# A gated MLP on one core: the early weights' queue, the way of the first products back into their banks, and the order of the operand sums

## The chip, the cores and the metric

The kernel runs on one core of a Trainium2 chip. The core has TensorE (PE, matrix products; its weight loads are shown as PEld), VectorE (DVE), ScalarE (ACT), GpSimd (POOL) and SyncE (SP), which here only issues DMAs. Each engine works through its own instructions in program order, and semaphores tie them together. The metric is the device time of one execution in microseconds (us), from the first to the last instruction with what lies around them. The kernel before took 557.13 us, the median of 3 runs (556.48 to 557.19).

## What is computed

```python
# x: [1, 2048, 1024]   w_gate, w_up: [1024, 3584]   w_down: [3584, 1024]   all bf16
g = jnp.einsum("bsd,df->bsf", x, w_gate)
u = jnp.einsum("bsd,df->bsf", x, w_up)
h = gelu(g) * u                      # tanh form of gelu
out = jnp.einsum("bsf,fd->bsd", h, w_down)
```

## The kernel before

**Tiling.** The 2048 rows are done in two passes of 1024 (`NPASS`). In a pass the rows form two column halves `xT[0]` and `xT[1]` of 512 rows each, transposed, with the 1024 input features in eight blocks of 128 (`ko`). The 3584 hidden features form 28 blocks of 128, and two blocks make a unit: 14 units a pass. After the units of a pass, `down` multiplies by w_down.

**Seven products instead of eight.** A unit is a 2 x 2 by 2 x 2 block product: two feature blocks by two halves of the weights' inner dimension, against two such halves of x by two row halves. It is computed in Strassen's manner (Winograd's form) with seven products, for gate and up each. The operands of four of them are sums: of weights (`s1` to `s4`, `sa`, made by `sums_s`) and of x (`t1` to `t4`, `tb`, made by `sums_t`); `sa` and `tb` are casts by ScalarE. A product is four matmuls of 128 x 512 (`product`), so the five products of sums in `unit` are 40 matmuls for gate and up. The other two products take raw bf16 operands: the first, p1, uses the lower half of the inner dimension; the second is added to p1 in its bank and gives the block c11 directly, of which ScalarE's gelu and VectorE's multiplication (`times`) make one quarter of the unit's h. A copy of p1 is kept, because p1 is also part of the unit's other blocks.

**Banks.** PSUM has eight banks, used in four pairs (gate and up): E, K, C and F. In `unit` the first pair `e` takes the product s2 by t2; p1 has to be added to it. ScalarE copies the sum out as u2, then the product s3 by t3 is added to the bank, and so on. `c[i]` and `d` take the others; `p5` is ScalarE's copy of s1 by t1. For the units 0 to 5 of the first pass line 229 adds the kept p1 on VectorE; the other units find p1 in the bank already, because their raw products run in it.

```python
   225          for i in GU:
   226              product(e[i], s["s2"][i], t["t2"], p1 is not None)
   227          if p1:
   228              for i in GU:
   229                  dve(e[i], e[i], p1[i], ADD)
```

In the first pass u2 and p5 are stored over `xT[1]` (`spare0`), so they also wait until t2, t3 and tb have been made from it.

**The early units.** The first 40 us are laid out by hand (lines 484 to 569). Before `xT[1]` has arrived, PE can only do the two raw products of units 0 to 5, which need `xT[0]` and three weight blocks: `wa[0]` (units 0 and 1), `wa[2]` (2 and 3) and `wa[4]` (4 and 5). The sums of weights of these units need `wa[1]`, `wa[3]` and `wa[5]` as well. A weight block is 1 MB, two DMAs of 512 KB (gate and up). `xT[0]` is loaded plainly and transposed by PE (`turn`, four of them, each copied out of a bank), and `xT[1]` is loaded by eight transposing DMAs of 128 KB (`transposing`, line 476). Everything is issued on SP's queue, in this order: half of x's first rows, `wa[0]` in four slices with the other half of x between, `wa[2]`, four transposes, `wa[4]`, `wa[1]`, four transposes, `wa[3]`, `wa[5]`.

**The orders around the change.** PE, VectorE, GpSimd and SP keep the order of the program text everywhere, and so does ScalarE within the blocks under `manual_schedule`. The early block runs `early_p1` (first raw product), `early_snap` (ScalarE copies p1 out), `early_p2` (second raw product) and `early_c11` (gelu and multiplication), for units 0 and 1, then 2 and 3, then 4 and 5. Between them VectorE makes t1, s1, s2 (while GpSimd makes s3), then t2 and t3, and after the last c11 s4 and t4. `pool_behind` gives GpSimd a copy of one column of the last t3 tile, so that it starts on unit 1's sums only when t3 is done; `nxt = {"s": make_s(early[1], pool)}` are those sums. From then on GpSimd makes each unit's sums one unit ahead (`prepare`). VectorE meets unit 0's two additions of line 229 only after t4, since they stand behind it in the program.

**Names in the profile.** A bank shows as `bank`, the operands of sums as `s` and `t`, a copy of p1 as `p`. Copies over `xT[1]` show as `xT`, early data kept in the space of h as `hT` (among them `wa[3]` to `wa[5]`). Helpers give their line to all that they record: L91 is every VectorE sum, L94 every GpSimd sum, L108 every `snap`, L103 every `cast`, L115 every product, L127 every weight load, L194 every gelu.

Of the kernel before, what the change touches and what calls it, by code (L numbers as in the profile page):

```python
# [10 lines left out]
def kernel(  # L11
# [23 lines left out]
    nc = tc.nc  # L35
# [15 lines left out]
    NKB = Dm // P  # L51
# [8 lines left out]
    R = 6  # L60
# [29 lines left out]
    def dve(out, a, b, op):  # L90
        nc.vector.tensor_tensor(out=out, in0=a, in1=b, op=op)  # L91
# [29 lines left out]
    def new_w():  # L121
        return wpool.tile([P, 2, NKB, 2 * P], bf16, name="w")

    def load_w(n, w, k0=0, k1=NKB):
        f0 = n * 2 * P
        for i, src in enumerate((w_gate, w_up)):
            nc.sync.dma_start(  # L127
                out=w[:, i, k0:k1],
                in_=src[k0 * P : k1 * P, f0 : f0 + 2 * P].rearrange(
                    "(ko ki) f -> ki ko f", ki=P  # L130
                ),
            )
        return w
# [66 lines left out]
    def product(ps, lhs, rhs, start):  # L200
        for k in range(KH):
            matmul(ps, lhs[:, k, :], rhs[k], start and k == 0, k == KH - 1)
# [16 lines left out]
        g, up = add(c, p1)  # L219
        times(fb, 0, gelu(g), up)  # L220

    def unit(fbs, banks, s, t, p1, spare, after_p5, aside, keep, ahead_of_p4, behind_p4):
        GU = range(2)
        e, c, d = banks
        for i in GU:
            product(e[i], s["s2"][i], t["t2"], p1 is not None)
        if p1:
            for i in GU:
                dve(e[i], e[i], p1[i], ADD)
        aside()  # L230
        keep(0, c[0])
        u2 = [snap(e[i], "u2", spare[i]) for i in GU]
        keep(1, c[0])
        keep(2, c[1])
        up = c[1]
        c = d
        for i in GU:
            product(c[i], s["s1"][i], t["t1"], True)
        p5 = [snap(c[i], "p5", spare[2 + i]) for i in GU]
        after_p5()  # L240
        for i in GU:
            product(e[i], s["s3"][i], t["t3"], False)
        g = new(dve, e[0], p5[0], ADD, "sum", dtype=f32)
        dve(up, e[1], p5[1], ADD)
        for i in GU:
            product(c[i], s["s4"][i], t["tb"], False)
        times(fbs[1], 1, gelu(g), up)
        g, up = add(c, u2)
        times(fbs[0], 1, gelu(g), up)
        ahead_of_p4()  # L250
        for i in GU:
            product(e[i], s["sa"][i], t["t4"], False)
        behind_p4()
        times(fbs[1], 0, gelu(e[0]), e[1])
# [205 lines left out]
    def turn(ps, half, a, parts):  # L460
        tp = ps.bitcast(bf16).rearrange("p (k r) -> p k r", k=KH)
        for t in range(2):
            for k in range(KH):
                nc.tensor.transpose(
                    tp[:, k, t * P : (t + 1) * P], xn[half, a][:, t, k * P : (k + 1) * P], ident
                )
        n = KH // len(parts)
        for m, put in enumerate(parts):
            ks = slice(m * n, (m + 1) * n)
            put(  # L470
                out=xT[0][:, half * KH : (half + 1) * KH, a * 2 * P : (a + 1) * 2 * P][:, ks],
                in_=tp[:, ks],
            )

    def transposing(xT, c, ko, r0):
        nc.sync.dma_start_transpose(  # L476
            out=xT[c][:, ko, :], in_=x2[r0 : r0 + N, ko * P : (ko + 1) * P]
        )
# [7 lines left out]
    load_w(0, wa[0], 0, 2)  # L486
    load_w(0, wa[0], 2, 4)
    load_x(1)
    load_w(0, wa[0], 4, 6)
    load_w(0, wa[0], 6, 8)  # L490
    load_w(2, wa[2])
    for ko in range(KH):
        transposing(xT, 1, ko, N)
    load_w(4, wa[4])
    load_w(1, wa[1])
    for ko in range(KH, NKB):
        transposing(xT, 1, ko, N)
    load_w(3, wa[3])
    load_w(5, wa[5])
# [1 line left out]
    seen = xpool.tile([P, 1], f32, name="seen")  # L501
    E, K, C, F = odd, cc, dd, even
    s, t = sums_s(early[0], dve), sums_t(xT)
    s_pool = sums_s(early[0], pool)
    p1s = {}

    def early_p1(u, ps, i, ks, cols=slice(0, N)):
# [19 lines left out]
    def early_c11(u, ps):  # L527
        times(block(0, u, 0), 0, gelu(ps[0]), ps[1])

    with tc.manual_schedule(engines={ENG.Activation}):  # L530
        for _ in range(NWARM):
            nc.tensor.matmul(bank[3], lhsT=warm[:, :P], rhs=warm, start=True, stop=True)
        turn(bank[4], 0, 0, (on_dve,))
        turn(bank[5], 0, 1, (on_dve, on_act))
        pairs = [(u, ps, i) for u, ps in ((0, E), (1, K)) for i in range(2)]
        for cols in (slice(0, 2 * P), slice(2 * P, N)):
            for u, ps, i in pairs:
                early_p1(u, ps, i, range(0, 2), cols)
        for u, ps, i in pairs:
            early_p1(u, ps, i, range(2, KH))  # L540
        turn(bank[6], 1, 0, (on_dve,))
        turn(bank[7], 1, 1, (on_dve,))
        early_snap(0, E)
        early_snap(1, K)
        for ks in (range(0, 2), range(2, KH)):
            for u, ps, i in pairs:
                early_p2(u, ps, i, ks)
        early_c11(0, E)
        early_c11(1, K)
        for us in (((2, C), (3, F)), ((4, E), (5, K))):  # L550
            for u, ps in us:
                for i in range(2):
                    early_p1(u, ps, i, range(KH))
                early_snap(u, ps)
            if us[0][0] == 2:
                t.make("t1")
                s_pool.make("s3")
                s["s3"] = s_pool["s3"]
                s.make("s1", "s2")
            else:  # L560
                t.make("t2", "t3", "tb")
            for u, ps in us:
                for i in range(2):
                    early_p2(u, ps, i, range(KH))
                early_c11(u, ps)
        s.make("s4", "sa")
        t.make("t4")
        pool_behind(t["t3"][-1])
        nxt = {"s": make_s(early[1], pool)}
    spare0 = [as_f32(xT[1][:, 2 * m : 2 * m + 2]) for m in range(4)]  # L570

# [17 lines left out]
    for ip in range(NPASS):  # L589
        with tc.manual_schedule(engines={ENG.Activation}):  # L590
            if ip == 0:
                ws = {}
            else:
                raw_of(0, F)()
                raw_of(1, C)()
            for u in range(NU):
                js = making(u) if ip == 0 else []

                def prepare():
                    if "s" not in nxt and u + 1 < NU:  # L600
                        nxt["s"] = make_s(weights(ip, u + 1), pool)
                    if len(js) == 1:
                        store_made(js[0])
                    for j in js[1:]:
                        keep_whole(j)
                    if ip == 0:
                        fetch_wd(making(u + 1))

                def keep(part, ps):
                    if js:  # L610
                        keep_part(js[0], part, ps)

                def aside():
                    if u + 2 < NU:
                        weights(ip, u + 2)

                def ahead_of_p4():
                    if u % 2 and u + 1 < NU and (ip or u + 1 >= R):
                        raw_of(u + 1, F)()
                        nxt["c11"] = raw_of(u + 2, C)  # L620

                def behind_p4():
                    if "c11" in nxt:
                        nxt.pop("c11")()

                if u % 2 and (ip or u):
                    E, K, C = C, E, K
                banks = (E, K, C) if u % 2 else (F, K, E)
                unit(
                    [block(ip, u, h) for h in range(2)], banks, s, t,  # L630
                    p1s.pop(u) if ip == 0 and u < R else None,
                    [None] * 4 if ip else spare0,
                    prepare, aside, keep, ahead_of_p4, behind_p4,
                )
                s = nxt.pop("s", None)

        last = ip == NPASS - 1
        got, nxt = {}, {}

        def more(step):  # L640
            if last:
                return
            if step in (-1, 0, 2):
                store_made({-1: NJ - 3, 0: NJ - 2, 2: NJ - 1}[step])
            if step == 0:
                xT[:] = new_x()
            if step >= 24 and step % 2 == 0 and step // 2 - 12 < len(moves):
                c, ko = moves[step // 2 - 12]
                transposing(xT, c, ko, (2 * (ip + 1) + c) * N)
            if step == 50:  # L650
                ws.clear()
                loaded(0), loaded(1)
            if step == 58:
                got["s"] = make_s(loaded(0), dve)
            if step == 62:
                got["t"] = make_t(xT)

        down(ip, F + K, C + E, last, more)
        E, K, C, F = K, E, F, C
        if not last:  # L660
            t, s = got["t"], got["s"]
# [29 lines left out]
```

## Time and profile before

| what | value |
|---|---|
| median of 3 runs | 557.13 us (556.48 to 557.19) |
| the profiled execution's own time | 557.8 us |
| its span, first to last instruction | 556.0 us |
| mean granted clock of PE | 0.988 of full |
| PE busy | 537.0 us, 97%, 2380 matmuls |
| VectorE busy | 351.4 us, 63% |
| ScalarE busy | 265.5 us, 48% |
| GpSimd busy | 251.2 us, 45% |
| bytes moved | 93.29 MB, mean 168 GB/s |
| chain that ended last | PE 89%, VectorE 3%, SP's queue 3%, DMA 3% |

Busy times are for the whole span; what a stage is limited by has to be read from that stage's own rows. The profile cuts the span into 40 slices (13.9 us each) and gives each engine's busy share as a digit in tenths. A timeline row has the start, the time from the first start to the last end of the merged instructions, engine, line, operation, what is written and read, and the count; in brackets stands how long the engine had been idle before and what released it. A row `SPq` is the issue of a DMA, not its transfer. A row of waits has the total, the number of times and the longest.

### The profile page before, as it was taken

What the parts mean: (1) busy time and instruction counts of PE and PEld (TensorE: products, weight loads), DVE (VectorE), ACT (ScalarE), POOL (GpSimd) and SP (SyncE); (2) the same over time, 40 slices, a digit from 0 to 9 for tenths busy, and PEclk for the clock granted to TensorE, in tenths of its full rate; (3) what the DMA queues carried; (4) which work ended last, traced back from release to release, by engine and by line L of the source; (5) the groups of instructions that cost most, each with busy time, mean ns of one, the idle gap of its engine ahead of it and who ended that gap; (6) DMA issues with size and microseconds to landing.
All of it is one profiled execution on the core that took longest, in us unless ns stands there. A gap on an engine that the chain in (4) does not pass through costs nothing.

```text
span 556.0 us, 7452 instructions
## 1 busy us (share of the span) xinstructions
PE 537.0 (97%) x2380; PEld 386.2 (69%) x2399; DVE 351.4 (63%) x530; ACT 265.5 (48%) x471; POOL 251.2 (45%) x223
## 2 busy tenths in 40 slices
PE   8956999999999999999999999999999999999997
PEld 4434887686776864788877686867677686478886
DVE  1396787776776788478676546455455548866730
ACT  3523666676666631044535555645555552114541
POOL 0149997868776040000029776677777700000000
PEclk9986999999999999999999999999999999999999
DMA  9960059674846499999958242222222029662751
GB/s 235 209 161 17 23 176 259 170 217 132 265 126 209 141 367 386 292 251 215 282 180 212 65 107 77 76 77 77 77 76 77 1 80 382 239 219 87 222 194 56
DMA packets 108744, 93.29 MB, mean 168 GB/s; under 512 B 17313, under 2 KB 94113, under 8 KB 108705
## 3 DMA queue, kind: packets, MB, share of 16 engines
q1 hardware_dynamic: 108704, 92.82, 57.9%
q8 instruction: 19, 0.31, 0.3%
q14 instruction: 21, 0.16, 0.1%
HBM read 74.45 MB, written 15.20 MB: 161 GB/s over the span
## 4 chain that ended last, share of the span: by engine, by line
PE 89%; DVE 3%; SPq 3%; DMA 3%; issue 1%; ACT 0%; DVEq 0%; ACTq 0%
PE bank L115 89%; DVE t L91 2%; SPq L127 2%; DMA w<-in_w_up_dram 1%; SPq L476 1%; DMA raw<-in_w_down_dram 1%; DVE s L91 1%; DVE m L91 0%; DVE hT L91 0%; SPq L453 0%; ACT xT L108 0%; DVE bank L91 0%; ACT bank L281 0%; ACT st L422 0%; SPq L292 0%
## 5 line engine op out<-in xcount | busy, mean ns | idle before, releaser
L94 POOL TENSOR_TENSOR s<-w 128x512 fp32r<-128x512 bf16 x90 | 107.6, 1213 | 172.2 <-PE bank L115 100.2
L115 PE MATMUL bank<-t,s 128*128 128x512 f32 x672 | 161.4, 396 | 11.6 <-ACT xT L108 9.5
L115 PEld LDWEIGHTS bank<-t,s 128*128 128x128 f32 x672 | 127.8, 191 | 40.5 <-POOL s L94 10.4
L115 PE MATMUL bank<-xT,w 128*128 128x512 bf16 (+1 forms) x412 | 89.9, 375 | 2.2 <-DVE xT L470 1.0
L91 DVE TENSOR_TENSOR hT<-g,bank 128x512 bf16<-128x512 f32 x112 | 76.6, 688 | 18.8 <-ACT g L194 7.4
L194 ACT ACTIVATE g<-sum 128x512 f32<-128x512 f32 x78 | 49.5, 635 | 72.1 <-DVE sum L91 71.7
L108 ACT COPY p<-bank 128x512 f32<-128x512 f32 x96 | 54.6, 590 | 46.3 <-PE bank L115 45.8
L115 PEld LDWEIGHTS <-w 128*128 128x128 bf16 x424 | 40.4, 98 | 50.1 <-issue 4.1
L91 DVE TENSOR_TENSOR sum<-bank,p 128x512 f32<-128x512 f32 x36 | 24.9, 692 | 75.9 <-PE bank L115 75.9
L115 PE MATMUL bank<-q 128*128 128x512 f32 x240 | 58.9, 389 | 0.0
L115 PE MATMUL bank<-t,sa 128*128 128x512 f32 x224 | 57.5, 398 | 0.0
L115 PE MATMUL bank<-tb,s 128*128 128x512 f32 x224 | 56.4, 395 | 0.0
L94 POOL TENSOR_TENSOR s<-s,w 128x512 fp32r<-128x512 f32 x48 | 55.7, 1180 | 0.0
L94 POOL TENSOR_TENSOR s<-w,s 128x512 fp32r<-128x512 bf16 x48 | 55.7, 1181 | 0.0
L115 PEld LDWEIGHTS bank<-q 128*128 128x128 f32 x240 | 45.0, 188 | 9.4
L115 PEld LDWEIGHTS bank<-tb,s 128*128 128x128 f32 x224 | 42.8, 192 | 9.4 <-issue 0.3
L115 PEld LDWEIGHTS bank<-t,sa 128*128 128x128 f32 x224 | 42.1, 188 | 9.6
L115 PE MATMUL bank<-raw,hT 128*128 128x512 bf16 x218 | 48.4, 379 | 0.3
L103 ACT CAST tb<-raw 128x512 fp32r<-128x512 bf16 x28 | 17.3, 627 | 62.4 <-DMA raw<-in_w_down_dram 26.9
L115 PEld LDWEIGHTS <-hT 128*128 128x128 bf16 x256 | 24.8, 98 | 31.1 <-DMA hT<-in_w_up_dram 1.1
L108 ACT COPY xT<-bank 128x512 f32<-128x512 f32 x56 | 31.3, 589 | 23.3 <-DVE bank L91 18.1
L91 DVE TENSOR_TENSOR q<-hT 128x512 fp32r<-128x512 bf16 x56 | 38.4, 686 | 4.4 <-PE bank L115 4.4
(54 smaller groups left out, 539.5 us busy)
## 6 DMA issues: line engine op xcount, KB each, us to landing
raw<-in_w_down_dram SPq DMA_DIRECT2D x76, 256.0 KB, 5.0
q<-td SPq DMA_DIRECT2D x60, 256.0 KB, 5.0
w<-in_w_gate_dram SPq DMA_DIRECT2D x24, 512.0 KB, 5.7
w<-in_w_up_dram SPq DMA_DIRECT2D x24, 512.0 KB, 6.9
td<-m SPq DMA_DIRECT2D x12, 768.0 KB, 4.5
w<-td SPq DMA_DIRECT2D x6, 1024.0 KB, 9.9
out_dram<-st SPq DMA_DIRECT2D x32, 128.0 KB, 1.7
hT<-in_w_gate_dram SPq DMA_DIRECT2D x3, 512.0 KB, 5.5
```

Source lines behind the costliest of these rows:

```text
L91: nc.vector.tensor_tensor(out=out, in0=a, in1=b, op=op)
L94: nc.gpsimd.tensor_tensor(out=out, in0=a, in1=b, op=op)
L103: nc.scalar.copy(out=t, in_=src)
L108: nc.scalar.copy(out=t, in_=ps)
L115: nc.tensor.matmul(ps, lhsT=lhs, rhs=rhs, start=start, stop=stop, skip_group_check=True)
L127: nc.sync.dma_start(out=w[:, i, k0:k1], in_=src[k0 * P : k1 * P, f0 : f0 + 2 * P].rearrange("(ko ki) f -> ki ko f", ki=P),)
L194: nc.scalar.activation(g, src, ACT.Gelu_apprx_tanh)
L476: nc.sync.dma_start_transpose(out=xT[c][:, ko, :], in_=x2[r0 : r0 + N, ko * P : (ko + 1) * P])
```

## The change

Four things are edited. (1) The second half of `wa[0]`, and `wa[2]`, `wa[1]` and `wa[4]` whole, are issued by ScalarE (`queue=nc.scalar`), at four places between its copies and gelus; a one-column copy of x into `seen` makes ScalarE wait for the first x before the first of them. On SP the eight transposes follow each other directly behind x, then come `wa[3]` and `wa[5]`. (2) The turns of x's second half stand between PE's first products, and ScalarE takes half of the last one's copy. (3) The add of p1 in units 0 to 5 is dropped. A new function `seed` lets ScalarE copy p1 into the bank `e` ahead, for unit 0 at the end of the early block and for units 1 to 5 in the unit before, and the product is added to it. (4) s3 of unit 0 is made by VectorE and no longer by GpSimd; t3 and tb follow unit 4's c11; s3, s4, sa and t4 follow unit 5's; the call of `pool_behind` goes.

```diff
@@ -121,10 +121,10 @@
     def new_w():
         return wpool.tile([P, 2, NKB, 2 * P], bf16, name="w")
 
-    def load_w(n, w, k0=0, k1=NKB):
+    def load_w(n, w, k0=0, k1=NKB, queue=nc.sync):
         f0 = n * 2 * P
         for i, src in enumerate((w_gate, w_up)):
-            nc.sync.dma_start(
+            queue.dma_start(
                 out=w[:, i, k0:k1],
                 in_=src[k0 * P : k1 * P, f0 : f0 + 2 * P].rearrange(
                     "(ko ki) f -> ki ko f", ki=P
@@ -219,14 +219,11 @@
         g, up = add(c, p1)
         times(fb, 0, gelu(g), up)
 
-    def unit(fbs, banks, s, t, p1, spare, after_p5, aside, keep, ahead_of_p4, behind_p4):
+    def unit(fbs, banks, s, t, spare, after_p5, aside, keep, ahead_of_p4, behind_p4):
         GU = range(2)
         e, c, d = banks
         for i in GU:
-            product(e[i], s["s2"][i], t["t2"], p1 is not None)
-        if p1:
-            for i in GU:
-                dve(e[i], e[i], p1[i], ADD)
+            product(e[i], s["s2"][i], t["t2"], False)
         aside()
         keep(0, c[0])
         u2 = [snap(e[i], "u2", spare[i]) for i in GU]
@@ -486,14 +483,7 @@
     load_w(0, wa[0], 0, 2)
     load_w(0, wa[0], 2, 4)
     load_x(1)
-    load_w(0, wa[0], 4, 6)
-    load_w(0, wa[0], 6, 8)
-    load_w(2, wa[2])
-    for ko in range(KH):
-        transposing(xT, 1, ko, N)
-    load_w(4, wa[4])
-    load_w(1, wa[1])
-    for ko in range(KH, NKB):
+    for ko in range(NKB):
         transposing(xT, 1, ko, N)
     load_w(3, wa[3])
     load_w(5, wa[5])
@@ -501,7 +491,6 @@
     seen = xpool.tile([P, 1], f32, name="seen")
     E, K, C, F = odd, cc, dd, even
     s, t = sums_s(early[0], dve), sums_t(xT)
-    s_pool = sums_s(early[0], pool)
     p1s = {}
 
     def early_p1(u, ps, i, ks, cols=slice(0, N)):
@@ -527,26 +516,38 @@
     def early_c11(u, ps):
         times(block(0, u, 0), 0, gelu(ps[0]), ps[1])
 
+    def seed(u, e):
+        for i in range(2):
+            nc.scalar.copy(out=e[i], in_=p1s[u][i])
+
+    on_queue = nc.scalar
     with tc.manual_schedule(engines={ENG.Activation}):
         for _ in range(NWARM):
             nc.tensor.matmul(bank[3], lhsT=warm[:, :P], rhs=warm, start=True, stop=True)
+        nc.scalar.copy(out=seen, in_=xn[0, 0][:, 0, :1])
+        load_w(0, wa[0], 4, 8, on_queue)
         turn(bank[4], 0, 0, (on_dve,))
         turn(bank[5], 0, 1, (on_dve, on_act))
+        load_w(2, wa[2], queue=on_queue)
         pairs = [(u, ps, i) for u, ps in ((0, E), (1, K)) for i in range(2)]
         for cols in (slice(0, 2 * P), slice(2 * P, N)):
             for u, ps, i in pairs:
                 early_p1(u, ps, i, range(0, 2), cols)
-        for u, ps, i in pairs:
+        for u, ps, i in pairs[:2]:
             early_p1(u, ps, i, range(2, KH))
         turn(bank[6], 1, 0, (on_dve,))
-        turn(bank[7], 1, 1, (on_dve,))
+        early_p1(*pairs[2], range(2, KH))
+        turn(bank[7], 1, 1, (on_dve, on_act))
+        early_p1(*pairs[3], range(2, KH))
         early_snap(0, E)
         early_snap(1, K)
+        load_w(1, wa[1], queue=on_queue)
         for ks in (range(0, 2), range(2, KH)):
             for u, ps, i in pairs:
                 early_p2(u, ps, i, ks)
         early_c11(0, E)
         early_c11(1, K)
+        load_w(4, wa[4], queue=on_queue)
         for us in (((2, C), (3, F)), ((4, E), (5, K))):
             for u, ps in us:
                 for i in range(2):
@@ -554,18 +555,18 @@
                 early_snap(u, ps)
             if us[0][0] == 2:
                 t.make("t1")
-                s_pool.make("s3")
-                s["s3"] = s_pool["s3"]
                 s.make("s1", "s2")
             else:
-                t.make("t2", "t3", "tb")
+                t.make("t2")
             for u, ps in us:
                 for i in range(2):
                     early_p2(u, ps, i, range(KH))
                 early_c11(u, ps)
-        s.make("s4", "sa")
+                if u == 4:
+                    t.make("t3", "tb")
+        seed(0, F)
+        s.make("s3", "s4", "sa")
         t.make("t4")
-        pool_behind(t["t3"][-1])
         nxt = {"s": make_s(early[1], pool)}
     spare0 = [as_f32(xT[1][:, 2 * m : 2 * m + 2]) for m in range(4)]
 
@@ -619,6 +620,9 @@
                         raw_of(u + 1, F)()
                         nxt["c11"] = raw_of(u + 2, C)
 
+                    if ip == 0 and u + 1 < R:
+                        seed(u + 1, F if u % 2 else C)
+
                 def behind_p4():
                     if "c11" in nxt:
                         nxt.pop("c11")()
@@ -628,7 +632,6 @@
                 banks = (E, K, C) if u % 2 else (F, K, E)
                 unit(
                     [block(ip, u, h) for h in range(2)], banks, s, t,
-                    p1s.pop(u) if ip == 0 and u < R else None,
                     [None] * 4 if ip else spare0,
                     prepare, aside, keep, ahead_of_p4, behind_p4,
                 )
```

## The prediction

> **What bounds the kernel now.** I read the page first: TensorE (PE) is busy 97% of a 556.0 us span, so there is little to gain except where PE stands still. The slices show where that is.
>
> ```profile
> PE   8956999999999999999999999999999999999997
> PEclk9986999999999999999999999999999999999999
> ```
>
> Only slices 2 and 3 (about 28 to 56 us) are below 9 after the first; the granted clock falls there too. Waits of PE from 48 us to the end come next:
>
> ```profile
> PE bank L115 <- ACT xT L108: 0.3, 1, 0.3
> ```
>
> That is all: once unit 1 has begun, at 55.11 us in the order of time, PE runs dense, one unit per 9.07 us (55.11 to 64.18). So the end moves by as much as the start of unit 1 moves, unless something new makes PE wait later. The stretches of 5 us (PE, PEld, DVE, ACT, POOL busy, then granted clock, DMA share and GB/s) and the order of time show what holds unit 1:
>
> ```profile
> 30.00:35.00 5.00, 3.23 (x7) 2.01 (x8) 5.00 (x9) 2.49 (x5) 0.00 (x0) 0.71 1.08 288
> 40.00:45.00 5.00, 0.00 (x0) 0.00 (x0) 5.00 (x4) 0.00 (x0) 5.00 (x5) 0.73 0.00 0
> 45.00:50.00 5.00, 3.10 (x7) 2.48 (x8) 2.43 (x4) 3.40 (x7) 5.00 (x5) 0.50 0.00 0
> ```
>
> ```profile
> 39.23 6.30 DVE L91 TENSOR_TENSOR t<-xT,t 128x512 fp32r<-128x512 bf16 x4
> 41.84 3.15 POOL L94 TENSOR_TENSOR s<-w 128x512 fp32r<-128x512 bf16 x2
> 45.45 1.28 DVE L91 TENSOR_TENSOR bank<-bank,p 128x512 f32<-128x512 f32 x2
> 46.17 1.19 ACT L108 COPY xT<-bank 128x512 f32<-128x512 f32 x2 [13.69 <-DVE bank L91]
> 46.90 3.75 PE L115 MATMUL bank<-t,s 128*128 128x512 f32 x8 [9.20 <-ACT xT L108]
> ```
>
> The reader should see a queue, not a shortage. PE finished unit 0's first two products at 37.7. Its third waits for ScalarE's copy u2 of the first product, which waits for VectorE to add p1 to that bank (line 229), and this add stands in VectorE's order behind s4 and t4, which nobody needs yet. PE idles 9.20 us, and after that pause the clock is 0.50: the last 24 matmuls of unit 0 take 46.90 to 55.11 = 8.21 us where 24/40 of 9.07 = 5.44 are normal, 2.8 us lost.
>
> **The p1 path.** The 12 adds of units 0 to 5 (0.70 us each, 8.4 us of VectorE) go, and 12 ScalarE copies into the bank come (`seed`; copies to SBUF take 0.59 at L108, casts into a bank 0.59 at L281, so 7.1 us). In units 1 to 5 this is worth nothing: PE waits nowhere there for the adds. The copies lie ahead of the unit's last gelu, on a ScalarE that is busy 2.7 to 4.6 of each 5 us from 55 to 80 us; without that cover they cost up to 1.2 us a unit. In unit 0 the 9.20 us stall goes. What is late next: unit 0 cannot start before seed 0, and that stands on ScalarE behind the last early gelu and the four tb casts. The last gelu can begin some 0.5 us after PE's early work (tb 4 x 0.62 between two gelus 1.9 us apart), then 0.6 for gelu and 0.6 for a copy: 1.7 us.
>
> **The loads.** SP loses the second half of w0, and w2, w1, w4; ScalarE issues them as 8 DMAs. Units 4 and 5 need w4. What the two layouts do to the transfers is read from the early DMA rates, first the whole early part (0 to 38 us), then a full stretch (20 to 24 us):
>
> ```profile
> DMA packets 18018, 8.41 MB, mean 221 GB/s; under 512 B 4705, under 2 KB 18017, under 8 KB 18017
> DMA packets 2418, 1.21 MB, mean 304 GB/s; under 512 B 46, under 2 KB 2418, under 8 KB 2418
> ```
>
> ```profile
> 9.16 6.42 SPq L476 DMA_TRANSPOSE xT<-in_x_dram  x4
> 15.62 1.96 SPq L127 DMA_DIRECT2D hT<-in_w_gate_dram  x1
> 19.00 2.74 SPq L127 DMA_DIRECT2D w<-in_w_up_dram  x1
> ```
>
> All early bytes (x 2.1 MB, six weight blocks 6.3 MB) arrive by 38 us, at 221 of a possible 304 GB/s. The holes lie around the transposes: SP spends 6.42 us on issuing four of them, and from 16.9 to 18.2 the DMA view shows 7 GB/s. With a second queue the holes can be filled. From 5 us on, when 0.75 MB are in, 7.64 MB at 304 GB/s take 25.1 us: everything is in at 30.1, with 1.4 us left for holes 31.5 us. But the order is worse for PE: w4 now goes out on ScalarE behind four p1 copies, a table load (1.28) and two gelus, at about 19 us, and shares the engines with w1, w3 and w5. Before, w4 was issued at 15.62 and 17.63 and in at 21.1 and 23.5. Bounds for the landing of w4: 26 us (issued at 19, 7.1 us to landing as for w2's second half) and 38 (the rate of before). I take 31.5, since both queues' last blocks end together when they share evenly.
>
> The Trainium skill, "DMA: Bandwidth & Descriptors", section "Issuing engines are not separate DMA queues", says that DMAs from several issuers interleave on the same 16 engines and that a second issuer saves only issue time. This speaks against the edit where the engines are full (20 to 24 us) and not where SP's issue leaves them at 7 GB/s; by the rule alone nothing lands earlier, and the total is that of rival C.
>
> The issue itself: on SP 0.47 us with a free queue, up to 2.74 when three blocks of 512 KB are outstanding. No ScalarE issue is in this trace, so 8 issues hold ScalarE 4 to 22 us; I take 0.6 each, as most of SP's, because only two blocks are outstanding on ScalarE at a time. The two of w1 push the table load and the first gelus back, and with them t1; cover: t1 and s1 must be followed by s2, which waits for w1 anyway (it landed at 26.9; I expect 24 to 25). Without that cover each us there is one us of VectorE's chain. The turns split between PE's first products, the half copy given to ScalarE and the late x1 (which now shares with w0) delay PE about 2 us at 12 us; that is hidden, because PE then waits for w4.
>
> **The end of PE's early work.** After w4's second half, 28 bf16 matmuls remain (u4's up product, u5's first pair, both second pairs), 0.224 each (47 in 10.52 us): 6.3 us. Before this PE has done units 2 and 3 by about 25 us and has then only four matmuls in 6 us; as after the pause of before I count 2.5 us of half clock. Early work ends at 31.5 + 6.3 + 2.5 = 40.3; it was 29.8.
>
> **VectorE's order.** s3 (2 x 0.62) comes from GpSimd, t3 moves behind c11 of unit 4, s3, s4 and t4 to the end. GpSimd loses s3 and the wait for t3 (`pool_behind`, 0.18 us): it starts unit 1's sums as w1 lands, at about 25 instead of 36.03, and then unit 2's. The row that prices this is t4 above: 6.30 / 4 = 1.575 us beside GpSimd, t3 alone 2.48 / 4 = 0.62. Only 0.95 us for each of VectorE's sums that meets one of GpSimd's, nothing for those that read a bank (0.69 in both cases). From the last c11 product at about 41.9 (40.3 + 0.3 + gelu 0.6 + 0.7) eight sums s3, s4, t4 remain: 5.0 us with none meeting, 12.6 with all. Unit 1's eight sums are over by about 34, and unit 2's want slots of unit 0; I take three meetings: 41.9 + 5.0 + 2.9 = 49.8. Then t4's last tile still has five matmuls behind it, 1.1: 50.9.
>
> The Trainium skill, "SBUF — State Buffer", section "SBUF: two separate sides", calls the port pair of VectorE and GpSimd an exclusive lock: the loser waits for the other's whole instruction. The row agrees in kind and is milder (1.575 against 0.62 + 1.15 = 1.77 by the rule); with all eight meeting, the rule would make the eight sums 14.2 us, and the total 1.6 us above rival B's.
>
> **The sum.** PE's path: 40.3 + 1.7 to seed 0 + 9.07 for unit 0 = 51.1; VectorE's path ends at 50.9, so both are near. Unit 1 starts at 51.1 instead of 55.11: 4.0 us earlier. Units 1 to the end stay as they are; the small pause at 94.3 to 95.5 (0.7 us of weights' load for sums, from a late w_down load) stays. The profiled execution took 557.8 us (span 556.0 and 1.8 around it): 553.8. The median of the runs shown is 557.13, 0.67 lower: 553.1.
>
> **Rivals.** A: w4 lands near 26, without the half clock. Early work ends at 32.3 and unit 0 at 43.1; VectorE's last sums then meet unit 2's on GpSimd, which ends them between 40 and 47.7. Middle: unit 1 at 45.5, total 557.13 - 9.6 = 547.5. For it: 304 GB/s in every full stretch. Against: w3 and w5 are issued by SP from about 16 us, ahead of w4.
> B: all eight sums meet GpSimd: 41.9 + 12.6 + 1.1 = 55.6, so 557.6, no change. For it: nothing holds GpSimd back any more. Against: it has done eight of its sums by then.
> C, the slower side: the holes do not fill, because the eight transposes in one run hold the engines or ScalarE's issues stand in a full queue (2.74); w4 lands with the last byte, as late as 38 us. Unit 1 starts at 38 + 6.3 + 2.5 + 1.7 + 9.07 = 57.6: 2.5 us later, 559.6. It decides from a landing at 35.5 us on.
>
> **Numbers.** Forecast 0.50 (its own range 550.5 to 556.0), A 0.22, B 0.15, C 0.13. The range must leave no more than 2 in 10 out, so it reaches from A's middle to just short of C: 547.5 to 559.0. Runs of this kernel differ by 0.1%, so 0.2% (1.1 us: below 556.0, above 558.2) is about what can be told from no change. Faster: 0.48 of the forecast, A's 0.22 and 0.03 of B = 0.73; the same: 0.02 + 0.09 of B and 0.01 of C = 0.12; slower: 0.03 of B and 0.12 of C = 0.15.
>
> **What would show it.** Right: ScalarE's wait of 13.69 us for the bank add is gone; no gap of 9 us on PE after unit 0's second product, a pause instead before u4's up product with a DMA of w4 as releaser; early DMA mean near 270 GB/s; the clock back at 1.00 by 45 us. Wrong: w4 in by 27 (A); t4 at 1.5 us each with PE waiting for it (B); w4 after 35 us, or ScalarE's issues above 1 us each with copies of banks late behind them (C); or new waits of PE for GpSimd's sums after 60 us, which would give back what the start won.

## The result, and the profile after

The changed kernel took 564.11 us (median of 6 runs, 560.36 to 565.9) against 556.95 for the kernel before beside it (6 runs): a ratio of 1.0124 with an interval of 1.0093 to 1.0155. It is slower by 7.1 us; the profiled execution took 564.88 with a span of 563.1. The forecast was 553.1 (547.5 to 559.0).

The slices of PE and of its granted clock, from the page:

```profile
PE   7786899999999999999999999999999999999997
PEclk9789799999999999999999999999999999999999
```

Slices 2 to 4 are still weak, and slices 0 and 1 have become weaker. PE's waits from 48 us on, and then the stretches of 5 us in the columns shown of before:

```profile
PE bank L115 <- DVE sum L91: 4.7, 1, 4.7
```

```profile
30.00:35.00 5.00, 4.98 (x16) 1.76 (x14) 2.27 (x3) 2.29 (x5) 2.23 (x2) 0.69 1.21 290
...
40.00:45.00 5.00, 3.85 (x19) 1.68 (x17) 5.00 (x5) 4.64 (x9) 3.37 (x3) 1.00 0.00 0
45.00:50.00 5.00, 4.33 (x19) 3.29 (x18) 5.00 (x8) 3.69 (x9) 1.56 (x1) 1.00 0.00 0
```

ScalarE's long stand and PE's 9 us of nothing between 40 and 50 are gone. VectorE is now full, GpSimd works beside it, and the new wait of PE, 4.7 us, is for a VectorE addition. Its other wait after 48 us, for s3, is 0.7 us. Followed backwards in the order of time, first PE:

```profile
16.91 10.01 PE L115 MATMUL bank<-xT,w 128*128 128x512 bf16 x32 [4.23 <-ACT p L108]
29.68 5.30 PE L115 MATMUL bank<-xT,w 128*128 128x512 bf16 x16 [2.77 <-ACT p L108]
35.74 1.04 PE L115 MATMUL bank<-xT,hT 128*128 128x512 bf16 x4 [0.76 <-DMA hT<-in_w_gate_dram]
37.28 6.22 PE L115 MATMUL bank<-xT,hT 128*128 128x512 bf16 x28 [0.51 <-DMA hT<-in_w_up_dram]
...
57.81 3.78 PE L115 MATMUL bank<-t,sa 128*128 128x512 f32 x8 [4.66 <-DVE sum L91]
```

The two rows with `hT` are units 4 and 5: w4 has landed at 35.7 and 37.3. The last row is unit 0's last product (sa by t4). Unit 1 starts at 61.39; it was 55.11. Now VectorE, and GpSimd beside it:

```profile
32.73 0.69 DVE L91 TENSOR_TENSOR s<-w 128x512 fp32r<-128x512 bf16 x1 [2.79 <-DMA w<-in_w_up_dram]
33.33 3.20 DVE L91 TENSOR_TENSOR s<-s,w 128x512 fp32r<-128x512 f32 x2
...
37.66 6.27 DVE L91 TENSOR_TENSOR t<-xT,t 128x512 fp32r<-128x512 bf16 x4
...
44.44 3.46 DVE L91 TENSOR_TENSOR t<-xT 128x512 fp32r<-128x512 bf16 x4
...
50.83 6.33 DVE L91 TENSOR_TENSOR t<-xT,t 128x512 fp32r<-128x512 bf16 x4
```

```profile
32.77 1.66 POOL L94 TENSOR_TENSOR s<-w 128x512 fp32r<-128x512 bf16 x1 [3.38 <-DMA w<-in_w_up_dram]
```

s1 waits for w1, which has landed at 32.7 (26.9 before); in the same moment GpSimd's sums of unit 1 are released by the same block (the first of them ran at 27.98, on w1's first half). s2, t2, one tile of t3 and t4 then run beside GpSimd: 3.20 for 1.28, 6.27 and 6.33 for 2.49, 3.46 for 2.49. Against the same sums alone that is 1.9 + 3.8 + 1.0 + 3.8 = 10.5 us. The loads behind it, ScalarE's issues and SP's:

```profile
13.78 0.37 ACTq L127 DMA_DIRECT2D w<-in_w_gate_dram  x1
15.37 0.38 ACTq L127 DMA_DIRECT2D w<-in_w_up_dram  x1
15.78 0.59 ACT L467 COPY xT<-bank 128x512 bf16<-128x512 bf16 x1 [9.07 <-DMA xT<-in_x_dram]
...
18.73 0.38 ACTq L127 DMA_DIRECT2D w<-in_w_gate_dram  x1
22.36 0.38 ACTq L127 DMA_DIRECT2D w<-in_w_up_dram  x1
...
23.95 0.98 ACTq L127 DMA_DIRECT2D hT<-in_w_gate_dram  x1
...
26.75 2.26 ACTq L127 DMA_DIRECT2D hT<-in_w_up_dram  x1
```

```profile
4.86 11.89 SPq L473 DMA_TRANSPOSE xT<-in_x_dram  x8
```

The pairs are w2, w1 and w4. ScalarE is free at 6.7 us, yet w2 goes out at 13.78; the copy of x at 15.78, whose data stood ready in the bank by 12.7, shows an idle time of 9.07 us "for xT". ScalarE stood at an issue, and behind it everything else: that copy, the copies of p1, and with them PE (4.23 and 2.77). Its three stands, at w2, w1 and w4, are 9.07, 4.44 and 3.90 us. The compiled program's list of ScalarE's instructions shows what an issue waits for:

```
L127 DMACopy w<-in_w_gate_dram [waits DMAHW4]
L127 DMACopy w<-in_w_up_dram [waits DMAHW6]
...
L127 DMACopy w<-in_w_gate_dram [waits DMAHW0]
L127 DMACopy w<-in_w_up_dram [waits DMAHW1]
...
L127 DMACopy hT<-in_w_gate_dram [waits DMAHW2]
L127 DMACopy hT<-in_w_up_dram [waits DMAHW3]
```

The DMAs of SP and ScalarE share eight completion semaphores in turn, and each issue waits until the DMA that had its semaphore last has landed. For w2 and w1 these are transposes of x on the other queue; for w4 they are the two halves of w3, issued at 16.80 and 17.42 and 7.1 and 9.3 us to landing: 23.9 and 26.7, to the tenth w4's issue times. So PE's next block was tied to one that nobody needed early. PE itself waits longer for ScalarE's copies (7.0 us) than for w4 (1.3 us, the two rows with `hT`).

The bytes did not come sooner. DMA rates in the stretch 4 to 13 us, before and then after (columns as above):

```profile
4.00:13.00 9.00, 7.51 (x62) 4.83 (x61) 2.36 (x4) 3.92 (x6) 0.00 (x0) 1.00 1.06 287
```

```profile
4.00:13.00 9.00, 6.89 (x56) 4.38 (x54) 2.23 (x4) 0.59 (x1) 0.00 (x0) 1.00 1.15 206
```

From 26 to 30 us, 119 GB/s became 292: the holes of before are filled, and new ones stand at 4 to 13 us. By these rates the last full microsecond of the transfers is the 35th instead of the 37th.

### The profile page after: what moved, and what is told of

Same layout as the page of the kernel before. It is cut to its first block, busy times and chain, and to the rows that moved or that the text cites. A ratio compares the mean times of both kernels' runs of the same rounds, so it can differ in the third digit from the quotient of the medians.

```text
span 563.1 us, 7471 instructions
## 1 busy us (share of the span) xinstructions
PE 542.6 (96%) x2399; PEld 386.4 (69%) x2399; DVE 350.2 (62%) x520; ACT 271.2 (48%) x485; POOL 249.6 (44%) x220
## 4 chain that ended last, share of the span: by engine, by line
PE 90%; DMA 4%; DVE 3%; SPq 2%; issue 1%; ACT 0%; DVEq 0%
PE bank L115 90%; DVE t L91 3%; DMA w<-in_w_up_dram 2%; SPq L473 2%; DMA xT<-in_x_dram 1%; DMA w<-in_w_gate_dram 1%; DVE hT L91 0%; DVE s L91 0%; SPq L450 0%; DVE sum L91 0%; ACT st L419 0%; DVEq L91 0%
## 5 line engine op out<-in xcount | busy, mean ns | idle before, releaser
L94 POOL TENSOR_TENSOR s<-w 128x512 fp32r<-128x512 bf16 x88 | 103.1, 1189 | 179.9 <-DVE t L91 86.0
L115 PE MATMUL bank<-t,s 128*128 128x512 f32 x672 | 159.1, 392 | 1.8 <-ACT bank L521 1.1
L115 PE MATMUL bank<-xT,w 128*128 128x512 bf16 (+1 forms) x424 | 97.6, 389 | 7.1 <-ACT p L108 7.0
L194 ACT ACTIVATE g<-sum 128x512 f32<-128x512 f32 x78 | 49.5, 634 | 78.7 <-DVE sum L91 78.4
L91 DVE TENSOR_TENSOR sum<-bank,p 128x512 f32<-128x512 f32 x36 | 24.9, 692 | 77.8 <-PE bank L115 73.6
L115 PE MATMUL bank<-t,sa 128*128 128x512 f32 x224 | 59.3, 408 | 4.7 <-DVE sum L91 4.7
L103 ACT CAST tb<-raw 128x512 fp32r<-128x512 bf16 x28 | 17.3, 627 | 62.3 <-DMA raw<-in_w_down_dram 26.7
```

The costliest lines, as they stand in the source:

```text
L94: nc.gpsimd.tensor_tensor(out=out, in0=a, in1=b, op=op)
L103: nc.scalar.copy(out=t, in_=src)
L115: nc.tensor.matmul(ps, lhsT=lhs, rhs=rhs, start=start, stop=stop, skip_group_check=True)
L194: nc.scalar.activation(g, src, ACT.Gelu_apprx_tanh)
```

## The experiments

The theories, with the letters that the expectations use: **Q**, ScalarE's issues wait for landings on the other queue, so w1 and w4 come late and ScalarE's copies with them; **G**, the meetings of VectorE with GpSimd cost the rest; **D**, the blocks come late because transfers share the engines with w3 and w5. Each ratio is to the kernel before, timed on the same chip. Edit (2), the turns, was not run by itself; where the loads of before come back, so do the turns.

**One part alone, and all but one.** `loads_alone` has only edits (1) and (2):

```diff
-            nc.sync.dma_start(
+            queue.dma_start(
...
+        load_w(2, wa[2], queue=on_queue)
...
+        load_w(1, wa[1], queue=on_queue)
...
+        load_w(4, wa[4], queue=on_queue)
```

> The kernel before with the change's loads and turns alone (ScalarE issues the second half of w0, w2, w1, w4; transposes in one run); the additions of p1 and the order of the sums as before, GpSimd held until t3. Theory Q (queue): ScalarE's issues wait for DMAs of SP that hold the same one of eight completion semaphores, so ScalarE stands still from 6.7 to 15.8 us, w1 lands at about 32.7 instead of 26.9 us, and with it all of VectorE's chain is 5.8 us later: 562.5 us (561 to 565). Theory G (GpSimd beside VectorE): GpSimd is held here, so there is little loss: 556 to 559 us.

Measured: 565.78, ratio 1.0172 (1.015 to 1.0195), 0.8 us above Q's range. The loads alone cost 9.4 us, more than the whole change. `loads_undone` is the changed kernel with the loads and turns of before:

> The changed kernel with the loads, queue and turns of before; seeds, new order of the sums and free GpSimd kept. Theory Q: w1 lands at 26.9 us again, VectorE's chain is 5.8 us earlier, unit 1 starts near 55.5: 557.5 us (556 to 559.5). Theory G: the 10 us that VectorE's sums lose beside GpSimd are still there and are the whole loss: 562 to 565 us.

Measured: 553.08, 0.9941 (0.9922 to 0.996), below both theories, which had left out what the seeds win. `seed_alone` has only edit (3), and GpSimd still held until t3:

```diff
-        if p1:
-            for i in GU:
-                dve(e[i], e[i], p1[i], ADD)
...
+        seed(0, F)
...
+                    if ip == 0 and u + 1 < R:
+                        seed(u + 1, F if u % 2 else C)
```

> The kernel before with the additions of p1 replaced by ScalarE's copies into the bank, nothing else. Theory Q: the 9.2 us pause of TensorE shrinks to the wait for the sums that follow t4 on VectorE (t4 ends at 45.5): unit 1 starts near 49.5 and the time is 551 us (549.5 to 553). Rival (the pause only changes its name, since unit 0's next additions also stand behind t4): 555 to 557 us.

Measured: 552.56, 0.9933 (0.9911 to 0.9955): 3.8 us won. The new way of p1 is good by itself; the loads are what is slow. In `seed_alone` unit 1 starts at 49.09, after a new wait:

```profile
45.79 3.16 PE L115 MATMUL bank<-t,sa 128*128 128x512 f32 x8 [4.37 <-DVE sum L91]
```

So even there the last product of unit 0 waits for VectorE, whose t4 takes 6.34 us beside GpSimd.

**GpSimd held.** `hold_pool` is the changed kernel with GpSimd's first sums behind t4:

```diff
+        pool_behind(t["t4"][-1])
         nxt = {"s": make_s(early[1], pool)}
```

> The changed kernel with GpSimd held until VectorE has made the last t4 tile (a copy of one column of it). Theory Q: w1 is still late (32.7), the chain of VectorE is shorter by the meetings with GpSimd (10 us), but unit 1 then waits for GpSimd's s1 and s2, four sums of 1.15 us after t4: 557.5 us (555 to 560). Theory G: all of the loss was the meetings: 552 to 555 us.

Measured: 557.16, 1.0015 (1.0003 to 1.0028). 7.0 us of the loss were meetings. VectorE, PE and ScalarE's issues of w4 in this kernel:

```profile
47.88 2.49 DVE L91 TENSOR_TENSOR t<-xT,t 128x512 fp32r<-128x512 bf16 x4
```

```profile
31.60 4.97 PE L115 MATMUL bank<-xT,w 128*128 128x512 bf16 x16 [6.34 <-ACT p L108]
36.41 7.07 PE L115 MATMUL bank<-xT,hT 128*128 128x512 bf16 x32
44.62 5.73 PE L115 MATMUL bank<-t,s 128*128 128x512 f32 x24 [1.14 <-ACT bank L521]
...
54.32 5.75 PE L115 MATMUL bank<-t,s 128*128 128x512 f32 x24 [0.34 <-ACT bank L521]
```

```profile
22.76 4.68 ACTq L127 DMA_DIRECT2D hT<-in_w_gate_dram  x1
27.48 3.44 ACTq L127 DMA_DIRECT2D hT<-in_w_up_dram  x1
```

t4 is 2.49, PE runs through unit 0 without the wait, and unit 1 starts at 54.32. What is left of the loss, against kernels with the old loads, lies before 44.62. There PE waits 10.7 us for ScalarE's copies of p1 (4.40 behind w2's issues, 6.34 behind w4's) and not at all for w4, whose halves land at 35.1 and 36.6, just as PE comes to them. Part of ScalarE's stand is the issue itself: w4's first one goes out as w3's first half lands (22.76 and 22.74) and then takes 4.68 us; the second, whose holder of the semaphore had landed at 24.7, goes out only behind it and takes 3.44 (`loads_alone`: 4.84 and 3.28). What makes an issue this long is not shown.

**Where the loads are issued.** `w2_early` issues w2 directly behind w0:

```diff
         load_w(0, wa[0], 4, 8, on_queue)
+        load_w(2, wa[2], queue=on_queue)
...
-        load_w(2, wa[2], queue=on_queue)
```

> The changed kernel with w2's two issues put directly behind those of w0 on ScalarE, ahead of its copies; nothing else. Theory Q (ScalarE's issues wait for landings of SP's DMAs and hold its copies up): ScalarE's copy of x's last half no longer waits 9.1 us, the second products start near 14 instead of 16.9 us, w1's second half is issued near 19 instead of 22.4 and lands near 29 instead of 32.7, and VectorE's chain with it: 560.5 us (558.5 to 562.5). Theory D (the transfers are the limit: w1 shares the engines with w3 and w5, which SP issues from 16.8 us): w1 does not land before 31.5: 562.5 to 565.5 us.

Measured: 562.27, 1.01 (1.0077 to 1.0123), at the upper end of Q's range. w2's first half now goes out at 6.29, its second stands until 10.80, and the copy of x's first half behind it starts at 11.26 instead of 6.12. The wait has moved along ScalarE, and s1's second half still waits for w1 until 30.1. `sp_w1` has the same and puts w1 and w4 on SP:

```diff
+    load_w(1, wa[1])
+    load_w(4, wa[4])
     load_w(3, wa[3])
```

> As w2_early, and w1 and w4 issued by SP behind the transposes and ahead of w3 and w5; ScalarE issues only w0's second half and w2. Theory Q: little more than w2_early, since w1 is issued at about 17.5 instead of 19: 559 us (557.5 to 561). Theory D: w1 no longer shares with w3 and w5, it lands at 24 to 25, 8 us earlier than in the changed kernel, and w4 at about 29: 555.5 us (553.5 to 557.5).

Measured: 555.69, 0.9981 (0.997 to 0.9992). w1 goes out at 16.44 and lands at 24.5, PE's early work ends at 38.7. The time is D's, and below Q's range. `pool_queue` lets GpSimd issue the eight DMAs:

```diff
-    on_queue = nc.scalar
+    on_queue = nc.gpsimd
```

> The changed kernel with the same loads issued by GpSimd instead of ScalarE; GpSimd has no other work before 25 us and its DMAs have completion semaphores of their own, so that nothing waits for SP's. Theory Q: all of w0, w2, w1, w4 are issued by 12 us, ScalarE is free, w1 lands by 22: 554 us (550 to 557). Theory D: the same bytes on the same engines, x and the transposes come later by what the weights take, w1 not before 27: 558 to 563 us.

Measured: 558.68, 1.0037 (1.0025 to 1.0049). That is in D's range and above Q's. None of GpSimd's issues waits, the last of w4 goes out at 7.49, and the price appears elsewhere:

```profile
4.84 21.34 SPq L473 DMA_TRANSPOSE xT<-in_x_dram  x8
```

With all blocks in flight at once the eight transposes take SP 21.34 us, t1 starts at 27.42 and the rest of the chain follows. Early issue alone was no gain here: what is needed first came later. t4 again took 6.34.

**The seeds with GpSimd held.** `seed_hold_t4` is `seed_alone` with the hold moved from t3 to t4:

```diff
-        pool_behind(t["t3"][-1])
+        pool_behind(t["t4"][-1])
```

> The kernel before with seeds (as seed_alone), and GpSimd held until t4 instead of t3. If the meetings of t4 with GpSimd (6.34 us for four instead of 2.48) are what holds unit 0's last product: t4 ends near 41.2 instead of 45.1, unit 1 then waits for GpSimd's s1 and s2, 4.6 us later: unit 1 starts near 46, 3 us earlier than seed_alone: 549.5 us (548 to 551). Rival (GpSimd's later start is given back in units 1 and 2): 552 to 554 us.

Measured: 546.91, 0.9825 (0.9805 to 0.9844), 1.1 us below the expected range, the lowest median of all and faster than both kernels. VectorE and PE:

```profile
38.20 2.48 DVE L91 TENSOR_TENSOR t<-xT,t 128x512 fp32r<-128x512 bf16 x4
```

```profile
44.63 5.71 PE L115 MATMUL bank<-t,s 128*128 128x512 f32 x24 [1.19 <-ACT bank L529]
```

GpSimd starts at 40.88 instead of 36 and still ends unit 1's sums in time: PE waits for none of them, only 1.19 us for ScalarE's copy of p1 into the bank.

**Which wait makes the blocks late.** `w1_sp` moves only w1 to SP, ahead of w3 and w5; ScalarE still issues w0's second half, w2 and w4:

```diff
+    load_w(1, wa[1])
     load_w(3, wa[3])
...
-        load_w(1, wa[1], queue=on_queue)
```

> The changed kernel with w1 alone moved: SP issues it right behind the transposes, ahead of w3 and w5; ScalarE still issues w0's second half, w2 and w4 where the change puts them. Theory D (what costs is w1's landing: issued late and sharing with w3 and w5): w1 lands at 24 to 25 us instead of 32.7, and the time falls by about 8 us: 556 us (554.5 to 558). Theory Q (what costs is that ScalarE stands still at w2's and w4's issues and its copies are late): little changes: 561 to 564 us.

Measured: 564.1, 1.0126 (1.0088 to 1.0163), as slow as the changed kernel, although w1 now goes out at 16.50 and 17.12 and lands at 24.6 and 26.5. ScalarE and PE show why:

```profile
24.64 0.38 ACTq L127 DMA_DIRECT2D hT<-in_w_gate_dram  x1
26.57 0.38 ACTq L127 DMA_DIRECT2D hT<-in_w_up_dram  x1
```

```profile
37.93 7.90 PE L115 MATMUL bank<-xT,hT 128*128 128x512 bf16 x28 [2.44 <-DMA hT<-in_w_up_dram]
```

w4 is issued as w1's two halves land, the holders of its semaphores now, and is complete at 37.9. PE's early work ends at 45.8, unit 5's c11 comes at 47.2, and t4, at 50.96, meets GpSimd's sums of unit 2 (6.33). So w1's landing, which D named for this run, is not by itself what holds the change: with w1 early, PE waits for ScalarE's copies (5.5 us) and for w4 (3.9). The time is Q's, but w4's issues are within 0.7 us of those in the change, and its transfers, 9.8 and 11.3 us (5.5 and 5.9 before), still share the engines with w3 and w5, which is D's cause. `w3w5_behind_w1` takes the sharing away instead; GpSimd issues w3 and w5 once w1 is in:

```diff
-    load_w(3, wa[3])
-    load_w(5, wa[5])
...
+        nc.gpsimd.tensor_copy(out=seen, in_=wa[1][:, 1, NKB - 1, :1])
+        load_w(3, wa[3], queue=nc.gpsimd)
+        load_w(5, wa[5], queue=nc.gpsimd)
```

> The changed kernel with w3 and w5 issued by GpSimd after w1 has landed (a one-column copy of w1 in front), not by SP behind the transposes; ScalarE's issues stand as in the change. If half of w1's delay is the sharing with w3 and w5: it is still issued at about 22 us, but takes 6 to 7 us instead of 10.3 and lands at 28.5 to 29.5: 560 us (558 to 561.5). If the late issue is all of it: 563 to 565 us.

Measured: 558.12, 1.0028 (1.0017 to 1.0039): 6 us back. w1 is in at 24.9, w4 at 29.5, PE's early work ends at 35.8, and then VectorE holds everything (t2 takes 6.19 us, t3 5.64, and t4):

```profile
44.66 6.33 DVE L91 TENSOR_TENSOR t<-xT,t 128x512 fp32r<-128x512 bf16 x4
```

This edit removes the sharing and changes which DMAs hold the semaphores too: w1 goes out at 13.41 and 15.16, not at about 22 as the expectation supposed. So its range was met by luck, and by itself the run does not part Q from D. `order_alone` is the kernel before with edit (4) only, the additions of p1 kept:

```diff
-                s_pool.make("s3")
-                s["s3"] = s_pool["s3"]
...
-                t.make("t2", "t3", "tb")
+                t.make("t2")
...
-        pool_behind(t["t3"][-1])
```

> The kernel before with the new order of the sums alone (s3 on VectorE, t3 and tb behind unit 4, s3, s4, t4 last, GpSimd not held); loads as before, additions of p1 kept. VectorE's chain is as in loads_undone, where t4 ended at 46.7 us, and the additions follow it, 1.3 us later than in the kernel before: 558 us (556.5 to 559.5). Rival (GpSimd's earlier start frees units 1 and 2): 553 to 556 us.

Measured: 560.81, 1.007 (1.0053 to 1.0087), 2.8 us above what was expected. t2 takes 6.26 and t4 4.39 beside GpSimd, the additions of p1 come behind them at 49.63, and PE waits 6.64 us for u2. So the new order without a hold costs 4.4 us by itself. `undone_hold_t4` is `loads_undone` with GpSimd held until t4:

> The changed kernel with the loads of before and GpSimd held until t4: seeds and the new order without any meeting of VectorE's sums and GpSimd's. t2 takes 2.5 us instead of 6.3, t4 ends near 41.5, unit 1 waits for GpSimd's s2 until about 46: 548 us (546.5 to 550). Rival (the meetings cost nothing in the end): 552 to 554 us as loads_undone.

Measured: 547.24, 0.9826 (0.981 to 0.9843). t2 takes 2.49, and unit 1 starts at 44.03. The ratio is that of `seed_hold_t4`: beside the seeds and the hold the new order adds nothing.

**Are these two causes all?** The last two kernels add the hold to `w3w5_behind_w1` and to `sp_w1`. Both keep the run of eight transposes and issues on ScalarE.

> The changed kernel with the two blocks that nobody needs early issued behind w1's landing, as in the earlier run, and GpSimd's first sums held until the last tile of t4. Theory L+G (the loss is the late landing of w1 and w4 and the meetings of VectorE with GpSimd, and nothing else of the edit costs): VectorE's t2, t3 and t4 take 2.49 us each, PE's early work ends at 35.8 as before, unit 0's second copies are in the banks at 36.9, 32 matmuls of 7.7 us and the last eight follow, unit 1 starts at about 46.6; against 44.63 in the kernel with the old loads held in the same way, which took 547.2, that is 549. Rival R (the run of eight transposes, the issues on ScalarE or the late second half of x cost something of their own that the meetings hid): unit 1 not before 50, 552.5 or more, with a wait of PE for ScalarE or for x.

Measured: 549.24, 0.9867 (0.9838 to 0.9896), 549 expected:

```profile
46.24 5.77 PE L115 MATMUL bank<-t,s 128*128 128x512 f32 x24 [0.33 <-ACT bank L519]
```

> The changed kernel with w1 and w4 on SP behind the transposes and ahead of w3 and w5, w2 directly behind w0 on ScalarE, and GpSimd's first sums held until the last tile of t4. Theory L+G: PE's early work ended at 38.7 in the run without the hold and is bounded by the landing of w4, so it stays; t1 and s1 no longer meet GpSimd (6.37 and 3.21 become 2.49 and 1.28); unit 1 starts at about 49.5, which is 552. Rival R: PE's start of unit 0 gets later or stays while another wait of PE before 40 us keeps the total above 554.5.

Measured: 551.42, 0.99 (0.988 to 0.9919), with unit 1 at 48.90; 552 and 49.5 expected. Both times are met to within a microsecond, but in this kernel not for the reason given. PE's early work is not bounded by w4:

```profile
15.01 1.86 PE L115 MATMUL bank<-xT,w 128*128 128x512 bf16 x4 [7.66 <-ACT xT L467]
```

From there to unit 1 neither PE nor VectorE waits for a weight block. PE waits for ScalarE's copy of x, which stands behind w2's issues (12.57 and 13.90), and the kernel is 4.2 us slower than `undone_hold_t4`. So the loss has three parts: ScalarE's stand at its issues, the late blocks, and the meetings.

The four kernels with the seeds and the new order, by loads (stand and late blocks together) and meetings:

| median, us | GpSimd free | GpSimd held until t4 |
|---|---|---|
| loads of before | 553.08 | 547.24 |
| loads of the change | 564.11 | 557.16 |

The loads cost 11.0 or 9.9, the meetings 5.8 or 7.0; the two hardly lean on each other.

## Why the prediction was wrong, step by step

**Held.** The end moves with the start of unit 1: span less that start is 500.9 before, 501.7 after, and 500.6 to 501.1 in the held kernels (545.4 - 44.63, 547.3 - 46.24, 554.9 - 54.32). Unit 0's stall of 9.20 us for u2 is gone, for two bank copies of 1.11 us together; alone that is worth 3.8 us. The meeting's price held: 6.33 / 4 = 1.58. The 28 matmuls behind w4 took 6.22, for 6.3.

**"I take 0.6 each ... because only two blocks are outstanding on ScalarE."** That was 4.8 us for eight issues. ScalarE stood for 17.4 us (9.07, 4.44 and 3.90), within the 4 to 22 that the prediction had named and then set aside. The issues themselves took 0.37 to 0.44, later 0.98 and 2.26 (up to 4.84 in `loads_alone`, which is C's sign). What the step left out is the wait in front of them, for a landing on the other queue: 7 us before w2. No row of before could show it, since all DMAs stood on one queue there.

**"With a second queue the holes can be filled", everything in at 31.5.** The last bytes came at about 36 us for 37. The holes around the transposes moved to the front (206 GB/s from 4 to 13 us for 287), because ScalarE stood where it should have issued. The Trainium skill, "DMA: Bandwidth & Descriptors", section "Issuing engines are not separate DMA queues", holds here: a second issuer saved at most issue time, and I set its rule aside for the holes. Here the second issuer also waited for the first one's landings, as the rows above show.

**"w1 ... 24 to 25" and w4 at 31.5.** 32.7 and 37.3. w4 alone is rival C, and its deciding point, 35.5, was passed. But C's price was too high and C alone would not have made the kernel slower: in `hold_pool`, with w4 in at 36.6 and no meetings, C's sum gives 56.2 (36.6 + 6.3 + 2.5 + 1.7 + 9.07), unit 1 starts at 54.32, since the half clock of 2.5 us does not come (PE's row behind w4 has 7.07 us for 32 matmuls), and 557.16 is within 0.2% of before.

**"I take three meetings."** It rested on unit 1's sums being over by 34, as w1 would land at 25. w1 landed at 32.7, so all but one of GpSimd's sums of unit 1 ran from 32.77 on, and with those of unit 2 they met eleven of VectorE's: 10.5 us for the 2.9 of the sum. B and C were priced as cases that exclude each other; the late block is the cause of both. B's "against" was the landing time that C denies.

**"Then t4's last tile still has five matmuls behind it, 1.1."** From t4's end, 57.16, to unit 1 it is 4.2 us. The last product also waits for VectorE's bank additions of unit 0, which stand behind t4, and after PE's pause of 4.66 us its eight matmuls take 3.78 for 1.98.

From unit 0's first seeded product at 44.65 a dense unit 0 ends at 54.3 (as `hold_pool` shows); 61.39 - 54.3 = 7.1 us is the meetings, the same that holding GpSimd gave back. Of the loads' part, Q's waits are shown by w4's first issue, which agrees to a tenth with the landing before it in four kernels (the change, `w1_sp`, `hold_pool`, `loads_alone`). How the 10 to 11 us divide between ScalarE's stand, the long issues and D's sharing with w3 and w5 was not separated: each run that took the sharing away also changed the holders of the semaphores.

## What to carry to other kernels

Before moving a DMA to another engine's queue, look up in the program what its issue waits for, and count what stands behind it on that engine; a completion semaphore that is reused ties two queues together, and an early block can so wait for one that nobody needs. When an engine's release is moved, list what it will then run beside, and price rivals that have one cause as one case. The gain here lay in a line that the change removed: holding GpSimd about 5 us longer (40.88 for 36.03), with the seeds, gives 546.91.

## What the runs showed of the hardware

Eight transposing DMAs of 128 KB held SP for 11.9 us in a run; with eight more DMAs that GpSimd had issued by 8.4 us, 21.3 us. A pause of PE costs afterwards too: unit 0's last eight matmuls took 1.97 us without one, 2.11 behind 0.8 us, and 3.06 to 3.78 behind pauses of 3.4 to 4.7 us, in no clear order within these. When VectorE and GpSimd both sum from SBUF, both slow down: VectorE's sums took 1.58 each (6.33 for four) and 0.62 alone (2.49), GpSimd's 1.58 (3.16 for two) and 1.15 alone (2.30). The issue of a 512 KB DMA took ScalarE from 0.37 to 4.84 us.
